# Three half-partition state copies moved from GpSimd to ScalarE in a recurrent-attention kernel

## The chip, the cores and the metric

The kernel runs on one core of a Trainium2 chip. Its time is the device time of one execution in microseconds (us). A core has five engines that run side by side and wait for each other through semaphores: TensorE (PE in the profile, with its weight loads as PEld), VectorE (DVE), ScalarE (ACT), GpSimd (POOL) and SyncE (SP), which here only issues DMAs. Each engine executes its own instructions in program order.

## The reference

A recurrence with a decaying state per batch and head runs over 768 tokens; its output, laid out as a 3072 x 384 matrix, goes through a maxout layer. Sizes: 4 batches, 8 heads, 48 numbers per head.

```python
for t in range(S):                       # _attn_ref, state is B x H x 48 x 48
    cur = np.einsum('bhd,bhe->bhde', u[None] * kt, vt)
    y[:, :, t] = np.einsum('bhd,bhde->bhe', rt, state + cur)
    state = wt[:, :, :, None] * state + np.einsum('bhd,bhe->bhde', kt, vt)

x = attn_out.transpose(0, 2, 1, 3).reshape(B * S, H * D)
out = np.maximum(x @ w1, x @ w2) @ w_out    # w1, w2: 384 x 1024, w_out: 1024 x 384
```

## The kernel before

The tokens are cut into three segments of 256. A **unit** is one or two batches at one segment: units 0 to 3 are the four batches at segment 0, one each; unit 4 is batches 0 and 1 at segment 1, unit 5 batches 2 and 3 at segment 1, units 6 and 7 the same at segment 2. A partition holds two neighbouring tokens.

For each unit `n` the steps, named as in the program, are these. `load` brings in r, k, v and the decays w by SP's queue. `wp` and `ln` form the logarithm of each pair's decay, `hi` and `lo` split it into two 16-bit parts (units 3 to 7), `ex` sums the logarithms over tokens by matmuls with a triangular matrix (the lines L380 and L381 are the two parts), `mz` adds a row's own, `e0` and `ie` are exponentials. `scale` multiplies r and k by them into `rp` and `kp`; `rw` and `kw` do the pairs' second factor. `tr` transposes these on TensorE and `te` copies the result out of PSUM into `RK` (units 5 to 7 use transposing DMAs, `dt`). `rk`, `ru`, `dg`, `dd` and `di` make the diagonal term: `rk` is the product of r and k (tile `rku`, L174 on VectorE, L178 on GpSimd, for unit 5 batch 0 on VectorE and batch 1 on GpSimd). `sc` makes scores in PSUM (L626), `mk` copies them under a mask into `M` (L635, VectorE), `ya` (L673) and `yi` (L660) make the output from the scores and from the state, `xe` copies it to `xT`.

The state: `kv` (L581) makes the segment's new key-value products in PSUM. `st.n.0` (L595 on ScalarE for segment 0, else L597 on VectorE) forms the state in the middle of the segment's pairs of halves, `st.n.1` (L600) a second sum `T`, and `sm` (GpSimd or VectorE) multiplies `T` by the decay `W` into the state for the next segment. `sb.n.e` (L606 to L610) converts the float32 state `S_f` to the bfloat16 `S_b` that `yi` uses as weights. It works on the partitions of one head of each pair: `e` = 0 is partitions 0 to 63, `e` = 1 partitions 64 to 127. So each of these copies has 64 partitions; from unit 4 on it is 768 numbers long, before that 192.

The maxout layer uses max(a, b) = b + relu(a - b): `gt` multiplies `xT` by w1 - w2 (L691), `rl` takes the relu out of PSUM into `gT` (L701 on ScalarE, L703 on VectorE), `op` adds the product with w2 w_out (L709) and that of `gT` with w_out (L713), `oe` copies the result to SBUF and `os` stores it. Units 0 to 3 have four `gt` blocks, units 4 to 7 eight.

PSUM has four banks under the tag G (`ex`, `tr`, `gt`, `op` take them in turn; a unit's `ex` keeps its bank until `scale` has read it) and two double banks under Y (`kv`, `sc`, the outputs `y`). A step that needs a bank waits for the release by the step that reads the bank's former contents.

What sets the order: the long string ORDER. Each word in it is one step, and each engine's instructions stand in the order of the words. `@a`, `@d` and `@p` name the engine of a step that can run on several: ScalarE, VectorE, GpSimd. Nothing is reordered by a scheduler; semaphore waits follow from the data.

Of the kernel before, what the change touches and what calls it, by code (L numbers as in the profile page):

```python
# [53 lines left out]
mz.0.1 e0.0.1 load.0.r rw.0.0@d ex.0.0 zero.M.1@p mz.0.0 ie.0.0 ie.0.1 kw.0.0@p identb@p wt.0.0  # L54
rw.0.1@p wt.0.1 load.1.w.0 u we.0.0 identq@a uspread hot.8.3 e0.0.0 wp.1.0@p ln.1.0 ex.1.0
zero.k.1@p rk.0.0@d utake@a ru.0.0@p load.1.r rw.1.0@p load.1.v vb.1.0@a zero.M.2@p load.0.v
scale.0.1.0.0@d scale.0.1.0.1@d scale.0.0.0.0@d tr.0.0.0 vb.0.0@a vb.0.1@a kv.0 st.0.0@a sb.0.0@p
scale.0.0.0.1@d tr.0.0.1 mz.1.0 ie.1.0 dg.0 dd.0@p we.0.1 load.1.k rk.1.0@d st.0.1 kw.1.0@d ru.1.0@d
wt.1.0 di.0.0@d te.0.0.0@a hot.8.5 sc.0.0.0.0 sc.0.0.1.0 we.1.0 vb.1.1@a te.0.0.1@a hot.8.4
sc.0.0.0.1 wload.1.2 w2turn.2.0 wload.0.1 e0.1.0 zero.M.0@p sm.0@p scale.1.0.0.0@d dg.1 load.2.w.0  # L60
# [17 lines left out]
ru.4.0@d scale.4.1.0.0@d tr.4.0.1 dg.4 sc.3.0.1.0 mk.3.0.1.0 sc.3.0.0.0 mk.3.0.0.0 oe.1.0@a  # L78
load.5.w.0 gt.2.0 rl.2.0@a load.3.v vb.3.1@a gt.2.3 rl.2.3@a gt.2.1 rl.2.1@a te.4.0.1@a vb.3.0@p
kv.3 st.3.0@a gt.2.2 scale.4.1.1.0@p kv.4 rl.2.2@a row.4 wp.5.0@p ln.5.0 hi.5@p dd.4@d di.4.0@d  # L80
di.4.1@d wl.3 load.5.r sb.3.0@a we.3 st.3.1 os.1.1 load.5.k sm.3@p os.0.1 load.5.v st.4.0 sb.4.0@p
rk.5.1@p ru.5.1@p tr.4.1.0 te.4.1.0@a tr.4.0.0 te.4.0.0@a op.0.0 tr.4.1.1 load.6.w.0 wp.6.0@p lo.5@d
st.4.1 rk.5.0@d ya.3.0.1.0 ex.5.1 ya.3.0.0.0 te.4.1.1@a sc.4.1.0.0 mk.4.1.0.0 sb.3.1@a yi.3.0
xe.3.0@a oe.0.0@a mz.5.1 ex.5.0 mz.5.0 op.2.1 oe.2.1@a sc.4.1.1.0 mk.4.1.1.0 sc.4.0.1.0 mk.4.0.1.0
# [18 lines left out]
xe.6.1@a ya.6.0.0.0 ya.6.0.1.0 op.5.0 scale.7.0.1.0@d dg.7 dt.7.0.1 xe.6.0@a gt.6.0 rl.6.0@d gt.6.1  # L103
rl.6.1@d gt.6.4 rl.6.4@a sm.5@p scale.7.1.1.0@p dt.7.1.1 scale.7.1.0.0@p gt.6.2 rl.6.2@d dd.7@d
vb.7.1@a gt.6.3 oe.5.0@a rl.6.3@a gt.6.6 gt.6.7 di.7.1@d rl.6.6@d gt.6.5 rl.6.5@d vb.7.0@a kv.7
st.7.0 sb.7.0@p sc.7.1.0.0 mk.7.1.0.0 rl.6.7@a op.6.0 sc.7.1.1.0 mk.7.1.1.0 dt.7.0.0 os.4.0 dt.7.1.0
op.6.2 sc.7.0.1.0 di.7.0@d mk.7.0.1.0 os.5.2 sc.7.0.0.0 mk.7.0.0.0 op.6.1 oe.6.1@d os.6.1 ya.7.1.0.0
ya.7.1.1.0 ya.7.0.0.0 ya.7.0.1.0 sb.7.1@a oe.6.0@d os.6.0 yi.7.0 yi.7.1 xe.7.0@a op.6.3 oe.6.3@a
os.6.3 os.5.3 os.5.0 oe.6.2@a xe.7.1@d gt.7.0 gt.7.7 rl.7.7@d rl.7.0@a gt.7.2 gt.7.1 rl.7.2@d gt.7.4
# [669 lines left out]
```

## Time and profile before

| | |
|---|---|
| three runs | 156.62, 158.8, 159.0 us; median 158.8 us |
| profiled execution, first to last instruction (span) | 156.0 us |
| its own time | not listed apart; the lowest of the runs lies 0.6 us above the span, the median 2.8 us |
| busy share of the span | PE 90%, DVE 80%, ACT 58%, POOL 58% |
| copies `S_b<-S_f` on ScalarE | 13: median 363 ns, longest 830 ns |
| copies `S_b<-S_f` on GpSimd | 3: 343, 817 and 1543 ns |

A row of the timeline gives start and length in us, engine, line, operation, output and inputs, their shapes, how many instructions are merged in the row, and in brackets how long the engine had been idle and what released it. A row of the chain gives start, length, engine, output and line. The shape `64x768` is partitions by elements. L166 is a helper that makes every plain copy and conversion, so its tile names tell which step it is. PEclk is the granted clock of TensorE as a share of full speed.

### The profile page before, as it was taken

Reading aid. Unit: us, or ns where it says so; the run is one execution under the profiler, and the core shown is the slowest. Engines: PE = TensorE matmul, PEld = TensorE weight load, DVE = VectorE, ACT = ScalarE, POOL = GpSimd, SP = SyncE. Lnnn points to the kernel's source line nnn. Section 1 sums busy time; section 2 is a strip of 40 time slices with the busy share of each in tenths; the row PEclk is TensorE's granted clock in tenths of the full one; section 3 lists DMA queues with packets and bytes.
Section 4 is the critical chain, followed back from the end, with each engine's and each line's share of the span. In section 5 each row is a group of like instructions: output and inputs, shape, how many; then the busy total and the mean of one; then the engine's idle time right before and its main releaser. Section 6 shows DMA issues by size and latency. Waiting matters only on the chain.

```text
span 156.0 us, 5548 instructions
## 1 busy us (share of the span) xinstructions
PE 140.7 (90%) x2401; PEld 85.9 (55%) x2404; DVE 124.1 (80%) x161; ACT 90.0 (58%) x165; POOL 90.4 (58%) x105
## 2 busy tenths in 40 slices
PE   4899987998899989793499999999999999999991
PEld 1364645666667758561365645665556646574560
DVE  4690997999979999499989995997889987854610
ACT  3253735779979896964069689544763673023111
POOL 7949389891734975599529579486099932000000
PEclk9999999999999999999779999999999999999998
DMA  4999997999999679996098399869989298024033
GB/s 107 305 299 365 312 327 234 326 284 344 266 244 280 169 175 334 220 254 190 1 218 238 66 194 237 228 182 152 264 195 252 52 135 200 4 103 153 0 128 131
DMA packets 71187, 31.85 MB, mean 204 GB/s; under 512 B 66293, under 2 KB 70390, under 8 KB 71162
## 3 DMA queue, kind: packets, MB, share of 16 engines
q1 hardware_dynamic: 71162, 31.49, 77.3%
q8 instruction: 19, 0.31, 0.9%
q14 instruction: 6, 0.05, 0.1%
HBM read 23.61 MB, written 4.73 MB: 182 GB/s over the span
## 4 chain that ended last, share of the span: by engine, by line
PE 63%; DVE 16%; ACT 6%; issue 5%; POOL 5%; DMA 3%; SPq 1%; DVEq 0%; POOLq 0%; ACTq 0%
PE G L691 19%; PE G L713 16%; PE G L709 7%; DVE rku L174 6%; PE Y L626 4%; PE G L232 3%; PE Y L673 3%; DMA lr<-in_r_dram 3%; DVE M L635 2%; PE Y L660 2%; ACT RK L166 2%; PE Y L581 2%; POOL wst L200 1%; PE G L305 1%; POOL kp L174 1%
## 5 line engine op out<-in xcount | busy, mean ns | idle before, releaser
L691 PE MATMUL G<-xT,wd_sb 128*128 128x256 bf16 (+1 forms) x192 | 35.3, 335 | 0.7 <-ACT xT L166 0.7
L713 PE MATMUL G<-wo_sb,gT 128*128 128x384 bf16 x192 | 35.1, 326 | 0.0
L635 DVE CAST_PREDICATED M<-mask,Y 128x1024 bf16<-128x1024 int32 (+1 forms) x26 | 28.9, 1135 | 3.7 <-PE Y L626 3.6
L701 ACT ACTIVATE gT<-G 128x512 bf16<-128x512 f32 x37 | 21.0, 603 | 18.4 <-PE G L691 18.4
L691 PEld LDWEIGHTS <-wd_sb 128*128 128x128 bf16 x192 | 18.8, 101 | 13.6 <-DVE M L501 0.7
L713 PEld LDWEIGHTS <-gT 128*128 128x128 bf16 x192 | 18.7, 98 | 12.5 <-ACT gT L701 0.2
L178 POOL TENSOR_TENSOR kp<-lk,iE 128x384 bf16<-128x384 f32 x16 | 18.2, 1161 | 8.3 <-issue 4.0
L232 PE MATMUL G<-S_b 128*128 128x512 bf16 x45 | 14.6, 469 | 2.2 <-DVE S_b L261 2.1
L178 POOL TENSOR_TENSOR rku<-rku,u_b 128x384 f32<-128x384 f32 x14 | 14.0, 1025 | 4.0 <-DVE rku L174 2.2
L166 ACT COPY osb<-G 128x384 f32<-128x384 f32 x17 | 8.1, 481 | 13.7 <-PE G L713 13.4
L709 PE MATMUL G<-wc_sb,xT 128*128 128x384 bf16 x72 | 15.7, 328 | 0.0
L166 ACT CAST xT<-Y 128x768 bf16<-128x768 f32 x10 | 10.1, 1020 | 9.8 <-PE Y L660 8.2
L174 DVE TENSOR_TENSOR rku<-lr,lk 128x768 f32<-128x768 f32 x9 | 15.3, 1712 | 0.0
L626 PE MATMUL Y<-RK 48*64 48x128 bf16 x384 | 9.8, 226 | 5.1 <-DVE M L635 4.5
L166 ACT COPY RK<-G 128x1024 bf16<-128x1024 bf16 x12 | 12.0, 1026 | 1.7 <-PE G L550 1.6
L626 PEld LDWEIGHTS <-RK 48*64 48x64 bf16 x384 | 6.3, 108 | 10.5 <-issue 9.9
L425 DVE TENSOR_TENSOR MZ<-G,lg 128x384 f32<-128x384 f32 (+1 forms) x13 | 6.7, 521 | 6.0 <-PE G L383 5.1
L174 DVE TENSOR_TENSOR rp<-lr,G 128x768 bf16<-128x768 f32 (+2 forms) x13 | 10.5, 824 | 0.9 <-ACT G L421 0.6
L487 DVE TENSOR_REDUCE dg<-rku 128x16 f32<-128x768 f32 x12 | 11.0, 946 | 0.0
L178 POOL TENSOR_TENSOR lk<-lk,lw 128x384 f32<-128x384 f32 x6 | 7.3, 1226 | 5.5 <-DVE rku L174 5.5
L703 DVE TENSOR_SCALAR gT<-G 128x512 bf16<-128x512 f32 x11 | 7.4, 690 | 3.8 <-PE G L691 3.8
L232 PEld LDWEIGHTS <-S_b 128*128 128x128 bf16 x48 | 5.0, 114 | 9.6 <-issue 4.4
(102 smaller groups left out, 241.1 us busy)
## 6 DMA issues: line engine op xcount, KB each, us to landing
lk<-in_k_dram SPq DMA_DIRECT2D x12, 384.0 KB, 5.8
lr<-in_r_dram SPq DMA_DIRECT2D x12, 384.0 KB, 6.4
lv<-in_v_dram SPq DMA_DIRECT2D x12, 384.0 KB, 6.4
out_dram<-osb SPq DMA_DIRECT2D x24, 192.0 KB, 2.1
lw<-in_w_dram SPq DMA_DIRECT2D x11, 384.0 KB, 5.1
gT<-in_moe_w_dram SPq DMA_DIRECT2D x4, 512.0 KB, 6.0
wso<-in_moe_w_out_dram SPq DMA_DIRECT2D x4, 384.0 KB, 6.0
wst<-in_moe_w_dram SPq DMA_DIRECT2D x2, 512.0 KB, 5.6
```

Of the source, the lines that this page charges most:

```text
L166: (nc.scalar.copy if e == "a" else nc.vector.tensor_copy if e == "d" else nc.gpsimd.tensor_copy)(o, i)
L174: op(o, a, b)
L178: op(o[:, g], a[:, g], b[:, g])
L232: nc.tensor.matmul(t, zz[:, 0:P], zz[:, 0:512], start=True, stop=True)
L487: nc.vector.reduce_sum(s.dg[:, b].rearrange("p i h -> p h i"), s.rku[:, b], axis=AX.X)
L626: nc.tensor.matmul(t[q * Q:(q + 1) * Q, e, p * P:(p + 1) * P].rearrange("s (i g) -> s i g", i=2), s.kT[d, b, j, y * n + p, q, :], s.rT[d, ...
L635: nc.vector.copy_predicated(t[:, :, 2 * n * y:2 * n * (y + 1)].rearrange("s i (p e) g -> s p e i g", e=2), mask[:, j].bitcast(I32).unsquee ...
L691: nc.tensor.matmul(t[:, m * n * P:(m + 1) * n * P].rearrange("c (b t) -> c b t", t=P), wd_sb[:, ko, fo * P:(fo + 1) * P], s.xT[:, 0:n, ko, :],
L701: nc.scalar.activation(o, i, AF.Relu)
L703: nc.vector.tensor_scalar_max(o, i, 0.0)
L709: nc.tensor.matmul(t[:, 0:HD], s.xT[:, a, ko, :], wc_sb[:, ko, :], start=(ko == 0), stop=False)
L713: nc.tensor.matmul(t[:, 0:HD], s.gT[:, c:c + P], wo_sb[:, f, :], start=False, stop=(f == FO - 1))
```

## The change

In ORDER the engine of `sb.0.0`, `sb.4.0` and `sb.7.0` is `@a` instead of `@p`. All other words, and their places, stay. `sb.0.1`, `sb.4.1` and `sb.7.1`, the same copies of the other 64 partitions, were on ScalarE already.

```diff
-scale.0.1.0.0@d scale.0.1.0.1@d scale.0.0.0.0@d tr.0.0.0 vb.0.0@a vb.0.1@a kv.0 st.0.0@a sb.0.0@p
+scale.0.1.0.0@d scale.0.1.0.1@d scale.0.0.0.0@d tr.0.0.0 vb.0.0@a vb.0.1@a kv.0 st.0.0@a sb.0.0@a
...
-di.4.1@d wl.3 load.5.r sb.3.0@a we.3 st.3.1 os.1.1 load.5.k sm.3@p os.0.1 load.5.v st.4.0 sb.4.0@p
+di.4.1@d wl.3 load.5.r sb.3.0@a we.3 st.3.1 os.1.1 load.5.k sm.3@p os.0.1 load.5.v st.4.0 sb.4.0@a
...
-st.7.0 sb.7.0@p sc.7.1.0.0 mk.7.1.0.0 rl.6.7@a op.6.0 sc.7.1.1.0 mk.7.1.1.0 dt.7.0.0 os.4.0 dt.7.1.0
+st.7.0 sb.7.0@a sc.7.1.0.0 mk.7.1.0.0 rl.6.7@a op.6.0 sc.7.1.1.0 mk.7.1.1.0 dt.7.0.0 os.4.0 dt.7.1.0
```

GpSimd's queue around `sb.4.0`, at the start of unit 5. The rows are, in turn, `hi.5` (output in the tile `wst`), `sm.3`, `sb.4.0`, and the GpSimd half of `rk.5` and `ru.5`; "x2" is one step in two instructions:

```order
 L200 TENSOR_SCALAR wst<-lg 128x768 [waits PE_49,Activation_49]
 L174 TENSOR_TENSOR S_f<-T,W 128x192 [waits DVE_49,Activation_49]
-L166 CAST S_b<-S_f 64x2x8x48 [waits DVE_49]
 L178 TENSOR_TENSOR rku<-lr,lk 128x384 [waits DMAHW7_49,DMAHW4_49]
 L178 TENSOR_TENSOR rku<-lr,lk 128x384
```

The copy of 64 partitions between `sm.3` and `rk.5.1` is gone; `rk.5.1` now stands right behind `sm.3`.

ScalarE's queue at the same place of the program. The rows are `sb.3.0`, `we.3` (the exponential that gives the decay `W`), the copy, the three `te.4` evictions into `RK`, and `sb.3.1`:

```order
 L166 CAST S_b<-S_f 64x4x48 [waits Activation_49]
 L473 ACTIVATE W<-WL 128x4 [waits DMAHW2_49]
+L166 CAST S_b<-S_f 64x2x8x48 [waits DVE_49]
 L166 COPY RK<-G 128x4x256 [waits PE_49] x3
 L166 CAST S_b<-S_f 64x4x48
```

`sb.4.0` now stands ahead of the three evictions and waits for VectorE's `st.4.0`.

ScalarE's queue around `sb.7.0`, where unit 6 ends its maxout and unit 7 has its new state. The rows are an `rl.6`, `vb.7.0` (the conversion of v), the copy `sb.7.0`, `rl.6.7`, `sb.7.1`, `xe.7.0` and an `oe`:

```order
 L701 ACTIVATE gT<-G 128x512 [waits PE_49]
 L166 CAST vp_77<-lv 128x8x2x48
+L166 CAST S_b<-S_f 64x2x8x48 [waits DVE_49]
 L701 ACTIVATE gT<-G 128x512 [waits PE_49]
-L166 CAST S_b<-S_f 64x2x8x48 [waits DVE_49]
+L166 CAST S_b<-S_f 64x2x8x48
 L166 CAST xT<-Y 128x6x2x64 [waits PE_49]
 L166 COPY osb<-G 128x384 [waits DMAHW3_49,DMAHW6_49,DVE_49,PE_49]
```

`rl.6.7` now stands behind a copy that waits for VectorE's `st.7.0`; before, it stood ahead of that wait.

## Prediction

> **What bounds the kernel now.** I read the chain that ended last first, for the engine that carries it; then the windows over the places where it leaves TensorE; then the timelines of the engines there.
>
> ```profile
> span 156.0 us, 5548 instructions
> ```
>
> The chain of waits in order of time (start, length, step). The pieces from 79.83 on are also my durations for TensorE at full clock:
>
> ```profile
> 68.13 6.77 DVE rku L174
> 74.90 1.14 DVE M L635
> 76.08 0.52 PE Y L626 x16
> 76.60 2.67 PE G L691 x12
> ...
> 79.83 1.42 PE G L691 x12
> 81.24 0.35 PE Y L673 x32
> 81.60 0.79 PE Y L660 x48
> 82.39 0.59 PE G L709 x3
> ...
> 90.25 0.63 PE Y L581 x64
> ...
> 151.44 1.31 PE G L713 x8
> ```
>
> From 76.08 to 152.75 the chain is TensorE's own work without a break: what delays or advances it there moves the end one for one. Before 76.08 stands one odd piece, a product on VectorE that took 6.77 us. The windows (length, busy time of each engine, granted clock) show what it does to TensorE:
>
> ```profile
> core 0: us, PE busy (x) PEld busy (x) DVE busy (x) ACT busy (x) POOL busy (x), PEclk, DMA share, GB/s
> 71.60:76.08 4.48, 0.01 (x3) 0.00 (x0) 4.48 (x3) 1.01 (x2) 3.58 (x5) 1.00 0.25 71
> 76.27:79.68 3.41, 3.41 (x44) 2.13 (x35) 2.95 (x4) 0.97 (x2) 0.67 (x1) 0.50 0.26 67
> ```
>
> TensorE stands for 4.48 us, and then works for 3.41 us at half clock. [...]
>
> Why the product is so long is read from the two queues, GpSimd's first, then VectorE's:
>
> ```profile
> 66.34 0.50 POOL L174 TENSOR_TENSOR S_f<-T,W 128x192 f32<-128x192 f32 x1
> 66.80 1.54 POOL L166 CAST S_b<-S_f 64x768 bf16<-64x768 f32 x1
> 68.31 1.96 POOL L178 TENSOR_TENSOR rku<-lr,lk 128x384 f32<-128x384 f32 x2
> ...
> 72.13 1.95 POOL L178 TENSOR_TENSOR lg<-lw 128x384 f32<-128x384 f32 x2
> 74.98 1.96 POOL L178 TENSOR_TENSOR lk<-lk,lw 128x384 f32<-128x384 f32 x2 [0.90 <-DVE rku L174]
> ```
>
> ```profile
> 66.40 1.26 DVE L398 SCALAR_TENSOR_TENSOR wst<-lg,wst 128x768 f16<-128x768 f32 x1 [2.27 <-POOL wst L200]
> 67.58 0.55 DVE L600 TENSOR_TENSOR T<-Y,S_f 128x384 f32<-128x384 f32 x1
> 68.05 6.85 DVE L174 TENSOR_TENSOR rku<-lr,lk 128x768 f32<-128x768 f32 x1
> ```
>
> ```profile
> L174 DVE TENSOR_TENSOR rku<-lr,lk x9: 947/955/6848, 7.7 to 113.2; 128x768 f32<-128x768 f32 x9
> L178 POOL TENSOR_TENSOR kp<-lk,iE x16: 987/999/1722, 28.8 to 125.3; 128x384 bf16<-128x384 f32 x16
> ```
>
> The product takes 0.955 us as a rule. Here it starts at 68.05, inside `sb.4.0`; GpSimd then runs six products without a gap until 72.13 + 1.95 = 74.08, and VectorE ends 0.82 us later, at 74.90. So it was shut out until GpSimd fell idle, which it did only because `kw.5` waits for this very product. [...]
>
> Elsewhere VectorE is not shut out so. Two pairs of products on GpSimd, each with the VectorE product that arrived during the pair's first:
>
> ```profile
> 56.07 2.78 POOL L178 TENSOR_TENSOR kp<-lk,iE 128x384 bf16<-128x384 f32 x2 [0.99 <-ACT iE L445]
> 56.23 1.76 DVE L174 TENSOR_TENSOR kp<-lk,iE 128x768 bf16<-128x768 f32 x1
> 80.91 2.68 POOL L178 TENSOR_TENSOR kp<-lk,iE 128x384 bf16<-128x384 f32 x2 [3.97 <-issue]
> 81.02 1.70 DVE L174 TENSOR_TENSOR rku<-rku,u_b 128x768 f32<-128x768 f32 x1
> ```
>
> Undisturbed, a pair takes 1.96 us. Here it takes 0.7 to 0.8 more, and VectorE about 0.75 to 0.8 more than its 0.955: it waits for the first product to end and goes next, and the second product waits for it. At 66.40 it also got in (between `sm.3`, which ends at 66.84, and `sb.4.0`, which took 1.54 instead of the 0.83 of a copy of that size). The one arrival that failed came during `sb.4.0`, the only GpSimd instruction in these rows that works on 64 partitions.
>
> [...]
>
> [...]
>
> **The change, part by part.** Three copies leave GpSimd and enter ScalarE, where the same copy of 768 numbers takes 0.83 us (a row below) and delays the next start by about 0.72.
>
> *At `sb.4.0`, GpSimd and VectorE.* `rk.5.1` follows `sm.3` directly. `lo.5` (66.40) still meets `sm.3`, gets in at 66.84 as before and ends at 67.66; `rk.5.1`'s first product is held until then and ends near 68.5. VectorE's `rk.5.0` arrives at 68.05 during this product, like the two arrivals above, gets in at 68.5 and ends near 69.3, **5.6 us earlier**. GpSimd saves the copy and pays one more hold of 0.8, so it is free at 74.0, as before.
>
> *TensorE behind it.* TensorE's last row ahead of its stand, which ends at 71.61:
>
> ```profile
> 71.19 0.42 PE L626 MATMUL Y<-RK 48*64 48x128 bf16 x16
> ```
>
> It then waits for `mk.4.1.0.0` (L635 at 74.90), which frees a double bank. That mask copy would now run from 69.3 to 70.4, before TensorE gets there, and the two `mz` after it end at 71.3. So TensorE goes on at 71.61 at full clock: scores 0.35, `gt` 1.33 to 1.42, scores 0.35, `gt` 1.42, `ya` 0.35, `yi` 0.79, in all 4.7. It would begin `op.3.0` at 76.3 instead of 82.39: **6.1 us**, of which 4.5 are the stand and 1.6 the half clock. What could be late next: the next `mk` needs scores that end at 71.6, and the four mask copies follow at 1.14 each: 72.8, 74.0, 75.1, each just ahead of the step that needs its bank (73.3, 75.1, 75.4). I take off 0.1 for these near meetings: 6.0.
>
> *What must move along.* VectorE, ScalarE and SP's queue (whose next row store waits for `mz.5`) follow these steps. GpSimd moves less: `kw.5` from 74.0 to 75.9, then four `kp` of 1.0, one conversion of v of 0.8 and two holds of 0.8: 82.3. `kv.5` needs them; TensorE comes to it at 90.25 - 6.0 = 84.2. So 1.9 us stay spare.
>
> *At `sb.4.0`, ScalarE*, with VectorE's `st.4.0` ahead:
>
> ```profile
> 63.59 0.55 DVE L597 TENSOR_TENSOR S_f<-Y,S_f 128x384 f32<-128x384 f32 x1
> ```
>
> ```profile
> 64.24 0.22 ACT L473 ACTIVATE W<-WL 128x4 f32<-128x4 f32 x1
> 64.58 1.93 ACT L166 COPY RK<-G 128x1024 bf16<-128x1024 bf16 x2
> 67.26 1.01 ACT L166 COPY RK<-G 128x1024 bf16<-128x1024 bf16 x1 [0.75 <-PE G L550]
> ```
>
> `st.4.0` is done at 64.14, so the new copy starts at 64.46 and the two evictions move by about 0.7. The third had waited 0.75 for TensorE: the delay ends there. Cost nothing; without that idle time it would be 0.7 for the evictions alone.
>
> *At `sb.0.0`.* ScalarE is without a gap here:
>
> ```profile
> 16.66 0.53 ACT L445 ACTIVATE iE<-MZ 128x384 f32<-128x384 f32 x1
> 19.39 0.52 ACT L421 ACTIVATE G<-G 128x384 f32<-128x384 f32 x1
> ```
>
> ```profile
> 20.13 0.55 DVE L174 TENSOR_TENSOR rp<-lr,G 128x384 bf16<-128x384 f32 x1
> 24.22 0.56 DVE L425 TENSOR_TENSOR MZ<-G,lg 128x384 f32<-128x384 f32 x1 [1.02 <-PE G L383]
> ```
>
> All of it moves by some 0.4. `e0.1.0` then ends at 20.3 instead of 19.9, and VectorE's `rp` starts 0.2 later; its idle 1.02 ahead of 24.22, which waits for another cause, takes that up. Cost nothing; at most the 0.4 if that idle time were not there.
>
> *At `sb.7.0`.*
>
> ```profile
> 128.61 0.62 ACT L701 ACTIVATE gT<-G 128x512 bf16<-128x512 f32 x1
> 130.33 0.83 ACT L166 CAST S_b<-S_f 64x768 bf16<-64x768 f32 x1 [1.10 <-DVE S_f L597]
> ```
>
> ```profile
> 130.29 1.46 PE L713 MATMUL G<-wo_sb,gT 128*128 128x384 bf16 x8
> ```
>
> `rl.6.7`, at 128.61 before, now waits for `sb.7.0`: start 130.33 + 0.72 = 131.05, end 131.67. It feeds the last of `op.6.0`'s eight matmuls, which started at 130.29 + 7 x 0.16 = 131.4 with its weights a little earlier. TensorE stands for **0.4 us**, and nothing behind gives it back. `sb.7.1` ends at 132.5, long before `yi.7`.
>
> **Sum**: 156.0 - 6.0 + 0.4 = 150.4 us of span. The runs lie 0.6 to 3.0 above the profiled span; the median 158.8 becomes 158.8 - 5.6 = **153.2**, the lowest 156.62 becomes 151.0.
>
> **Rivals.**
>
> *Shut out all the same.* If the cause lies in the two `rku` products or in a full GpSimd queue, and not in the copy, `rk.5.0` waits until GpSimd ends its six products. These end near 73.3 (one copy less, `lo.5`'s hold kept), so it ends 0.8 earlier. TensorE gains 0.8 and pays 0.4: 158.4. For it: six boundaries passed without letting VectorE in. Against it: both pairs above.
>
> *Something late takes part of the gain.* The mask copies or GpSimd's `kp` come late by 2 to 4 us in all: 155.2 to 157.2. Against it: the spare times above.
>
> *Slower: `lo.5` is shut out.* Without the copy, `sm.3` is followed by products. If VectorE does not get in at 66.84, it waits until GpSimd is idle at 66.8 + 6 x 0.96 = 72.6. Then `lo.5` ends at 73.4, and `ex.5.1` on TensorE, which needs it, stands from 67.7 (where `lo.5` ended before). The 3.9 us of work up to 71.6 would start at 73.4, 3.4 us of it at half clock: end 79.0, then 4.6 to `op.3.0` at 83.6 instead of 82.39. With 0.4 for `rl.6.7`: +1.6, 160.4; with a second such wait beyond 162. It decides at the end of `sm.3`. Against it: the same arrival got in before.
>
> **Chances.** Full gain 0.68 (own range 150.4 to 154.6); part of the gain 0.10; shut out all the same 0.12; `lo.5` shut out or other losses 0.10. A range from 150.4 to 158.5 takes in the first three cases and leaves about 0.15 out. About 2% is what a measurement of this kernel can tell from no change: faster takes the first case and a little of the second, 0.70; slower takes half of the last and a reserve for waits that I don't see, 0.09; the rest, 0.21, is the same.
>
> **What the profile after would show.** Right: `rk.5.0` about 1.7 us long, the first two GpSimd products of unit 5 about 0.7 longer each, no stand of TensorE near 72, no window at half clock there, and ScalarE's `rl.6.7` behind a copy near 125 with TensorE's short stand after it. Wrong: a VectorE product of several us at this place, or a new stand of TensorE in the stretch I moved as a whole.

## The result, and the profile after

| | before | changed |
|---|---|---|
| runs, us | 156.62, 157.66, 158.8, 159.0 | 152.03, 152.13, 152.38, 152.89 |
| median, us | 158.23 | 152.25 |
| profiled span, us | 156.0 | 150.3 |

The ratio of the times is 0.966, with a 95% interval from 0.959 to 0.973. A second series of the changed kernel gave a median of 151.73 and a ratio of 0.961 (0.954 to 0.969). Here and below, medians are of all runs, and ratios of the fast runs alone, those at most 1.5% above the fastest of their kernel in that series.

The page's first line of the changed kernel, and the window (length, busy time of each engine, granted clock) in which TensorE stood before:

```profile
span 150.3 us, 5551 instructions
```

```profile
core 0: us, PE busy (x) PEld busy (x) DVE busy (x) ACT busy (x) POOL busy (x), PEclk, DMA share, GB/s
71.60:76.40 4.80, 4.80 (x153) 3.76 (x146) 4.57 (x5) 4.40 (x7) 4.80 (x6) 1.00 1.00 249
```

TensorE now works through it at full clock. Its timeline there (start, length), up to the first matmuls of `op.3.0`:

```profile
71.41 0.64 PE L626 MATMUL Y<-RK 48*64 48x128 bf16 x32
71.99 1.48 PE L691 MATMUL G<-xT,wd_sb 128*128 128x256 bf16 x12
...
76.31 0.66 PE L709 MATMUL G<-wc_sb,xT 128*128 128x384 bf16 x3
```

In the profile before, the first twelve `gt` matmuls took 2.74 us instead of 1.48, and `op.3.0` started at 82.32 instead of 76.31:

```profile
76.53 2.74 PE L691 MATMUL G<-xT,wd_sb 128*128 128x256 bf16 x12
82.32 0.66 PE L709 MATMUL G<-wc_sb,xT 128*128 128x384 bf16 x3
```

The queues of VectorE and GpSimd at the same place:

```profile
66.65 1.26 DVE L398 SCALAR_TENSOR_TENSOR wst<-lg,wst 128x768 f16<-128x768 f32 x1 [2.26 <-POOL wst L200]
...
68.30 1.29 DVE L174 TENSOR_TENSOR rku<-lr,lk 128x768 f32<-128x768 f32 x1
```

```profile
66.59 0.50 POOL L174 TENSOR_TENSOR S_f<-T,W 128x192 f32<-128x192 f32 x1
67.05 3.39 POOL L178 TENSOR_TENSOR rku<-lr,lk 128x384 f32<-128x384 f32 x2
70.41 1.96 POOL L178 TENSOR_TENSOR rku<-rku,u_b 128x384 f32<-128x384 f32 x2
```

VectorE's product takes 1.29 us instead of 6.85. It got in between GpSimd's first and second product, and this pair on GpSimd took 3.39 instead of 1.96 because it was held twice, once by `lo.5` and once by `rk.5.0`.

The other end of the account is `sb.7.0`. ScalarE's and TensorE's timelines around `op.6.0`:

```profile
124.34 0.83 ACT L166 CAST S_b<-S_f 64x768 bf16<-64x768 f32 x1 [1.60 <-DVE S_f L597]
125.08 0.59 ACT L701 ACTIVATE gT<-G 128x512 bf16<-128x512 f32 x1
```

```profile
124.30 1.75 PE L713 MATMUL G<-wo_sb,gT 128*128 128x384 bf16 x8
```

The eight matmuls take 1.75 us instead of 1.46: the last waits for `rl.6.7`, which stands behind the copy.

The last eight matmuls, before and then after, end TensorE's work:

```profile
151.28 1.46 PE L713 MATMUL G<-wo_sb,gT 128*128 128x384 bf16 x8
```

```profile
145.63 1.46 PE L713 MATMUL G<-wo_sb,gT 128*128 128x384 bf16 x8
```

The account by the profiles: from the start of `rk.5.0` (68.05 before, 68.30 after) to `op.3.0` TensorE needs 8.0 us instead of 14.3, 6.3 less. The way up to there is 0.25 longer, and the way from `op.3.0` to the last matmul 0.36 longer (147.09 - 76.31 = 70.78 against 152.74 - 82.32 = 70.42), of which 0.3 lie in `op.6.0`. In all 5.7 us.

### The profile page after: what moved, and what is told of

Its sections match the earlier page's. It is cut to its first block, busy times and chain, and to the rows that moved or that the text cites. A ratio compares the mean times of both kernels' runs of the same rounds, so it can differ in the third digit from the quotient of the medians.

```text
span 150.3 us, 5551 instructions
## 1 busy us (share of the span) xinstructions
PE 138.8 (92%) x2404; PEld 84.3 (56%) x2404; DVE 118.5 (79%) x161; ACT 91.6 (61%) x168; POOL 89.8 (60%) x102
## 4 chain that ended last, share of the span: by engine, by line
PE 56%; DVE 18%; DMA 7%; POOL 6%; issue 5%; ACT 3%; SPq 3%; DVEq 0%; POOLq 0%; ACTq 0%
PE G L713 17%; PE G L691 16%; PE G L709 7%; DMA lr<-in_r_dram 7%; PE Y L673 4%; DVE M L635 3%; PE Y L626 3%; PE Y L660 2%; DVE dg L487 2%; PE G L232 2%; DVE rku L174 2%; SPq L357 2%; DVE kp L174 2%; DVE wst L398 2%; DVE rp L174 2%
## 5 line engine op out<-in xcount | busy, mean ns | idle before, releaser
L691 PE MATMUL G<-xT,wd_sb 128*128 128x256 bf16 (+1 forms) x192 | 34.1, 326 | 0.7 <-ACT xT L166 0.7
L691 PEld LDWEIGHTS <-wd_sb 128*128 128x128 bf16 x192 | 18.2, 98 | 13.0 <-DVE M L501 0.7
L709 PE MATMUL G<-wc_sb,xT 128*128 128x384 bf16 x72 | 15.7, 328 | 0.0
L166 ACT CAST S_b<-S_f 64x192 bf16<-64x192 f32 (+1 forms) x16 | 9.4, 589 | 1.8 <-DVE S_f L597 1.6
L174 DVE TENSOR_TENSOR rku<-lr,lk 128x768 f32<-128x768 f32 x9 | 9.7, 1092 | 0.0
L673 PE MATMUL Y<-M,vp 64*32 64x128 bf16 x768 | 9.1, 219 | 0.4 <-DVE M L635 0.4
```

What stands on the lines that cost most here:

```text
L166: (nc.scalar.copy if e == "a" else nc.vector.tensor_copy if e == "d" else nc.gpsimd.tensor_copy)(o, i)
L174: op(o, a, b)
L673: nc.tensor.matmul(lhsT=s.vp[g, b, 2 * p + e, j, m * 32:(m + 1) * 32], rhs=s.M[b, j][g, :, 2 * p + e, :], **into(s, b, q, p * 96 + (e + m) ...
L691: nc.tensor.matmul(t[:, m * n * P:(m + 1) * n * P].rearrange("c (b t) -> c b t", t=P), wd_sb[:, ko, fo * P:(fo + 1) * P], s.xT[:, 0:n, ko, :],
L709: nc.tensor.matmul(t[:, 0:HD], s.xT[:, a, ko, :], wc_sb[:, ko, :], start=(ko == 0), stop=False)
```

## Experiments

**Which of the three copies.** In the first kernel `sb.4.0` alone goes to ScalarE, in the second the other two.

```diff
 first:   st.4.0 sb.4.0@p  ->  st.4.0 sb.4.0@a
 second:  sb.0.0@p  ->  sb.0.0@a ,  sb.7.0@p  ->  sb.7.0@a
```

> Of the three copies only `sb.4.0` goes to ScalarE. My theory (the whole gain is VectorE's product `rk.5.0`, which no longer waits for GpSimd to fall idle; `sb.7.0` costs 0.4): span 149.9, 0.4 below the changed kernel's 150.3, and `op.6.0` on TensorE without a stand; median near 151.9. Rival (each copy that leaves GpSimd brings a part): 153 to 155.

> The other two copies, `sb.0.0` and `sb.7.0`, go to ScalarE; `sb.4.0` stays on GpSimd. My theory: the long wait of `rk.5.0` stays (6.8 us), TensorE stands for 4.5 us before 76 and works at half clock after it, and `sb.7.0` adds 0.4: median 158.6 beside 158.2 of the kernel before. Rival (each copy brings a part): 155 to 157.

The first had a median of 150.53 us, and 151.72 when it ran again beside the changed kernel's 151.73; its profiled spans are 148.3 and 150.1. The 148.3 comes from ahead of the change: `rk.5.0` began at 66.45 there, 1.8 earlier than in its second profile, and from it to the end it is 81.8 us in both profiles, against 82.0 in the changed kernel and 88.0 in the kernel before. All of the gain is `sb.4.0`'s. The second had a median of 158.68 beside 158.63 of the kernel before. Its ratio, 1.007 to 1.022, would be a loss of 1.1 to 3.4 us, more than the 0.4 expected; its profiled span, 156.5, is only 0.5 above that of before, half of it ahead of `rk.5.0`, and the size of the loss stays open. Its rows (VectorE's product; the two windows of stand and half clock; `op.6.0`):

```profile
68.29 6.84 DVE L174 TENSOR_TENSOR rku<-lr,lk 128x768 f32<-128x768 f32 x1
```

```profile
71.80:76.30 4.50, 0.02 (x4) 0.00 (x0) 4.50 (x3) 1.01 (x2) 3.60 (x5) 1.00 0.14 39
76.50:79.90 3.40, 3.40 (x44) 2.12 (x35) 2.95 (x4) 1.06 (x2) 0.65 (x1) 0.52 0.30 76
```

```profile
130.52 1.76 PE L713 MATMUL G<-wo_sb,gT 128*128 128x384 bf16 x8
```

Long product, stand and half clock are all there, and the stretched `op.6.0` as well. The other two copies bring nothing, and the rows show the cost that was named for `op.6.0`. In the kernel before, GpSimd had no queue behind them: after `sb.0.0` (16.82) came one conversion and then 2.19 us of idle time, after `sb.7.0` (130.36) nothing. VectorE's product that arrived at 17.05, during `sb.0.0`, took 0.96 us.

**The stand in `op.6.0`.** The changed kernel with two words exchanged:

```diff
-st.7.0 sb.7.0@a sc.7.1.0.0 mk.7.1.0.0 rl.6.7@a op.6.0
+st.7.0 sc.7.1.0.0 mk.7.1.0.0 rl.6.7@a sb.7.0@a op.6.0
```

> The changed kernel, with `sb.7.0` behind `rl.6.7` in ScalarE's queue instead of ahead of it. My theory (TensorE's stand of 0.3 to 0.4 in `op.6.0` comes from `rl.6.7` waiting behind the copy): the stand goes, median 0.3 to 0.4 below the changed kernel's 152.25, so 151.9. Rival (the stand has another cause or is made up for later): 152.25 as it was.

Median 151.76 us. ScalarE's and TensorE's rows of this kernel:

```profile
122.25 0.62 ACT L701 ACTIVATE gT<-G 128x512 bf16<-128x512 f32 x1
123.97 1.68 ACT L166 CAST S_b<-S_f 64x768 bf16<-64x768 f32 x2 [1.11 <-DVE S_f L597]
```

```profile
123.93 1.46 PE L713 MATMUL G<-wo_sb,gT 128*128 128x384 bf16 x8
```

`rl.6.7` is out of the way before the wait, and the eight matmuls take 1.46 again. The cause of the 0.3 is shown by the rows; the times alone, which scatter by 1 us within a kernel, could not tell it. The comparison of the first kernel with the changed one in the same series was expected to show it too:

> The kernel with `sb.4.0` alone on ScalarE, beside the changed kernel on the same chip. If `sb.7.0` on ScalarE costs what TensorE's stand in the changed kernel's `op.6.0` shows (0.3), this kernel is 0.3 faster than the changed one; both near 151 to 152.

> The changed kernel beside the one with `sb.4.0` alone, on the same chip: 152.2, 0.3 slower than it.

The times did not show it: the medians, 151.72 and 151.73, are equal. In the profiles `op.6.0` takes 1.46 and 1.76.

**What it is about the copy.** Four kernels put one instruction back on GpSimd at the place of `sb.4.0`, in the changed kernel; its output goes to a tile that nobody reads.

```diff
 st.4.0 sb.4.0@a  +  copy     64 partitions x 768      (first)
                  +  copy    128 partitions x 768      (second)
                  +  copy     64 partitions x 48       (third)
                  +  product  64 partitions x 384      (fourth)
```

> The changed kernel, with a copy of 64 partitions x 768 put back on GpSimd at the place of `sb.4.0`; it goes to a tile that nobody reads. Every theory that puts the gain down to that copy: `rk.5.0` again 6.8 us long, TensorE's stand and the half clock are back, time near 158.5. If the gain came from ScalarE doing the copy: 152.

> As before this, but the copy has all 128 partitions, so the same length on GpSimd and twice the data. [...] Theory B (arrival during a copy shuts VectorE out): 6.8 us and 158.5.

> The changed kernel, with a short copy of 64 partitions x 48 on GpSimd at that place, over before `rk.5.0` arrives (it then arrives during the first product of `rk.5.1`). [...] Theory B (what counts is the instruction during which it arrives): `rk.5.0` 1.3 to 1.8 us, time near 152.4.

> The changed kernel, with a product of 64 partitions x 384 on GpSimd at the place of `sb.4.0`, into a tile that nobody reads. [...] Theory B (only copies do it): `rk.5.0` 1.3 to 1.8 us; time near 152.4.

The kernel before, in the same series, took 156.06 to 159.17 us in eight runs (median of all nine 157.96) and once 738.15. GpSimd's and VectorE's rows, one kernel after the other. The first, 64 x 768 (runs 156.95 and 159.51 us):

```profile
67.33 1.54 POOL L619 CAST wso<-S_f 64x768 bf16<-64x768 f32 x1
```

```profile
68.58 6.84 DVE L174 TENSOR_TENSOR rku<-lr,lk 128x768 f32<-128x768 f32 x1
```

The second, 128 x 768 (152.4 and 152.57 us):

```profile
66.79 1.54 POOL L619 CAST wso<-S_f 128x768 bf16<-128x768 f32 x1
68.31 2.67 POOL L178 TENSOR_TENSOR rku<-lr,lk 128x384 f32<-128x384 f32 x2
```

```profile
68.05 1.11 DVE L174 TENSOR_TENSOR rku<-lr,lk 128x768 f32<-128x768 f32 x1
```

The two copies take the same 1.54 us and are interrupted by `lo.5` in the same way, and VectorE's product arrives during both. After 64 partitions it is shut out for the whole run of products, after 128 it goes next. So neither the load on GpSimd nor the arrival during a copy is the cause; the number of partitions is.

The third, 64 x 48 (median 157.11 us of eight runs):

```profile
65.01 0.94 POOL L623 CAST wso<-S_f 64x48 bf16<-64x48 f32 x1
65.91 1.96 POOL L178 TENSOR_TENSOR rku<-lr,lk 128x384 f32<-128x384 f32 x2
```

```profile
66.26 6.25 DVE L174 TENSOR_TENSOR rku<-lr,lk 128x768 f32<-128x768 f32 x1
```

Here the copy was over at 65.95, and VectorE arrived at 66.26, during a product on all 128 partitions. It was shut out all the same, for as long as the products ran: the sixth ended at 71.69, VectorE's 0.82 later, at 72.51. What the half-partition copy does outlasts it.

The fourth, a product of 64 x 384 (156.01 and 158.92 us):

```profile
66.91 1.71 POOL L616 TENSOR_TENSOR wso<-S_f 64x384 f32<-64x384 f32 x1
68.59 2.67 POOL L178 TENSOR_TENSOR rku<-lr,lk 128x384 f32<-128x384 f32 x2
```

```profile
68.16 1.29 DVE L174 TENSOR_TENSOR rku<-lr,lk 128x768 f32<-128x768 f32 x1
75.14 7.32 DVE L174 TENSOR_TENSOR rku<-rku,u_b 128x768 f32<-128x768 f32 x1
```

The time was like that of the kernel before, so it is not only copies that cost it, but the place was another: `rk.5.0` went next, in 1.29 us, and the next product of VectorE, `ru.5.0`, was shut out for 7.32 us, in a place where the other kernels don't show it (1.09 to 1.75 us there). The half-partition product lasted 1.71 us, of which some 0.75 are `lo.5`'s hold, so about as long on 64 partitions as one of 384 numbers on 128 (0.98). Why `ru.5.0` and not `rk.5.0` was shut out behind it is not shown by these runs.

**A wait on GpSimd.** The kernel before, with one tiny copy more on GpSimd that must wait until an earlier GpSimd instruction is complete on all partitions: right behind `sb.4.0`, or four products later.

```diff
 first:   st.4.0 sb.4.0@p       + copy of S_b[:, one element], waits for sb.4.0
 second:  rk.5.1@p ru.5.1@p     + copy of rku[:, one element], waits for ru.5.1
```

> The kernel before, all three copies on GpSimd, with one more instruction right behind `sb.4.0`: a copy of one element per partition out of `S_b`, which waits until `sb.4.0` is complete on all partitions. GpSimd gets more to do, not less. [...] Theory B (VectorE is shut out because it arrives during a copy, whatever comes then): no change, 158.2. Theory C (GpSimd's load is what counts): 158.2 or more.

> The kernel before, with a copy of one element per partition on GpSimd behind `ru.5.1`, which waits until `ru.5.1` is complete on all partitions; it stands four products behind `sb.4.0`. [...]

The first had a median of 151.98 us, ratio 0.969 (0.955 to 0.984). Its rows:

```profile
67.05 1.54 POOL L166 CAST S_b<-S_f 64x768 bf16<-64x768 f32 x1
68.66 0.80 POOL L624 COPY dum<-S_b 128x1 bf16<-128x1 bf16 x1
```

```profile
68.30 1.10 DVE L174 TENSOR_TENSOR rku<-lr,lk 128x768 f32<-128x768 f32 x1
```

The copy of the state is still on GpSimd, GpSimd has more to do than before, and the whole gain is there. The second had a median of 155.92 us, ratio 0.987 (0.979 to 0.994):

```profile
69.77 1.94 POOL L178 TENSOR_TENSOR rku<-rku,u_b 128x384 f32<-128x384 f32 x2
71.77 0.80 POOL L624 CAST dum<-rku 128x1 bf16<-128x1 f32 x1
```

```profile
67.58 4.94 DVE L174 TENSOR_TENSOR rku<-lr,lk 128x768 f32<-128x768 f32 x1
```

VectorE's product is shut out until the place of the wait, 71.71, and ends 0.81 later, at 72.52. Since it began 0.47 earlier than in the kernel before, this answers to 73.0 there, 1.9 ahead of its 74.9, as long as two of the six products (1.95). The wait's place sets the length of the shut-out. A tiny copy without a wait was not run; that the wait, and not just one more instruction, lets VectorE in rests on the six products that did not.

Whether the half clock goes with the shorter wait is read from TensorE's rows; it does not (line numbers here are 18 higher from the added code, so L644 makes scores and L709 is `gt`):

```profile
73.71 0.55 PE L644 MATMUL Y<-RK 48*64 48x128 bf16 x16 [2.60 <-DVE M L653]
74.19 2.74 PE L709 MATMUL G<-xT,wd_sb 128*128 128x256 bf16 x12
```

TensorE stood for only 2.60 us, and the twelve matmuls took 2.74 all the same.

**The half clock by itself.** The kernel before, with 16 matmuls more on TensorE in the time for which it stood; nobody reads their result.

```diff
-sc.4.1.1.0 mk.4.1.1.0 sc.4.0.1.0
+sc.4.1.1.0 hot.16.9 mk.4.1.1.0 sc.4.0.1.0
```

> The kernel before (all three copies on GpSimd, `rk.5.0` shut out as before), with 16 matmuls more on TensorE behind `sc.4.1.1.0`; their result is read by nobody, and they fill some 3.5 us of the 4.5 us for which TensorE stands. My theory of the sum (of the 6.1 us at `op.3.0`, 4.5 are the stand and 1.6 the half clock behind it): the product still ends near 74.9 and TensorE still goes on at 76.1, but at full clock, so `op.3.0` begins 1.6 earlier, near 80.7; time about 1.6 below the kernel before. Rival (half clock there has another cause or hides behind VectorE): `op.3.0` at 82.4 and no change.

The median of ten runs was 156.34 us, 0.8 below the 157.11 of the kernel before; the ratio was 0.983 (0.976 to 0.990), a gain of 1.5 to 3.8 us. TensorE's rows (15 of the 16 matmuls are in the profile):

```profile
70.94 3.63 PE L232 MATMUL G<-S_b 128*128 128x512 bf16 x15
75.51 0.42 PE L626 MATMUL Y<-RK 48*64 48x128 bf16 x16 [0.95 <-DVE M L635]
75.86 1.48 PE L691 MATMUL G<-xT,wd_sb 128*128 128x256 bf16 x12
77.58 0.42 PE L626 MATMUL Y<-RK 48*64 48x128 bf16 x16 [0.23 <-DVE M L635]
...
80.63 0.66 PE L709 MATMUL G<-wc_sb,xT 128*128 128x384 bf16 x3
```

With TensorE busy, the twelve `gt` matmuls behind the wait take 1.48 us instead of 2.74: the half clock is gone. From the start of `rk.5.0` (67.47) to `op.3.0` it is 13.16 us instead of 14.27, so 1.1 earlier, not 1.6. At full clock TensorE runs up to VectorE's mask copies, as the wait of 0.23 at 77.58 shows. In the changed kernel, where these come early, this loss doesn't occur.

How long the half clock lasts differs between executions with the same long wait. The kernel with the short added copy (64 x 48), from the end of TensorE's last matmul before its stand on (the granted clock is the third number from the right):

```profile
69.80:71.80 2.00, 0.00 (x0) 0.00 (x0) 2.00 (x1) 0.99 (x2) 1.89 (x2) 1.00 0.40 115
71.80:73.70 1.90, 0.00 (x2) 0.00 (x1) 1.90 (x3) 0.00 (x0) 1.11 (x2) 0.50 0.04 10
73.70:78.60 4.90, 4.90 (x50) 3.23 (x50) 4.10 (x5) 2.04 (x3) 0.85 (x1) 0.50 0.54 141
```

Here the clock fell 2.0 us after the last matmul, inside the stand, and 4.9 us of work ran at half clock, as in the kernel with the 64 x 768 copy. In the kernel before it fell only when TensorE had begun again, and 3.4 us of work were slow. What sets the moment isn't shown by these runs.

## Why the prediction was right, by its steps

**The long wait of `rk.5.0`.** It was forecast to end near 69.3, and ended at 69.59 after a start 0.25 later; its length and the 3.39 us of GpSimd's pair are those of an arrival that goes next, 1.3 and two holds. (The prediction's list of signs said about 1.7 us, which does not follow from its own 68.05 to 69.3.) That the copy's 64 partitions were the cause was an inference from a single case. The half and full copies show that it is the number of partitions, the short copy that the effect outlasts the instruction, and the two added waits that it ends where GpSimd waits for its own earlier instruction. `rk.5.0` took 1.1 to 1.3 us when it went next, and 4.9 to 6.9 us when it was shut out behind a half-partition instruction with further products queued. What keeps it out for so long, no run shows.

**TensorE behind it.** Forecast: 6.1, less 0.1; measured from profile to profile at `op.3.0`: 82.32 - 76.31 = 6.0. Counted from the start of the product it is 6.3, since the changed kernel came there 0.25 later. The stand was 4.5 of it, and the rest, 1.8, is near the 1.6 set down for the half clock; taken alone, the half clock was worth 1.1. The size of this term was in part luck: in the two profiles where the half clock covers 4.9 us of work it would be larger (from `rk.5.0` to `op.3.0` it is 14.9 us with the 64 x 768 copy, against 14.3 in the kernel before, after stands of 4.43 and 4.47). How long a stand must be for the clock to fall is not shown; half clock stood behind stands of 4.47 us in the kernel before and 2.60 in the one with the later wait, and full clock behind 0.95 with TensorE kept busy. The steps that were to follow did: the three masks behind the scores run at 71.88 in one row, and nothing on TensorE waits for GpSimd later.

**ScalarE at `sb.4.0`** and **at `sb.0.0`.** At `sb.4.0` the copy ran at 64.60 and the delay of the evictions ended before TensorE's work. At `sb.0.0` VectorE's idle time ahead of the `MZ` row was 1.02 before and is 0.80 now, as if the 0.2 foreseen had been taken up:

```profile
24.87 0.56 DVE L425 TENSOR_TENSOR MZ<-G,lg 128x384 f32<-128x384 f32 x1 [0.80 <-PE G L383]
```

But it was 0.69 in the second profile of the kernel with `sb.4.0` alone, where `sb.0.0` is on GpSimd, so the row does not show it. The start of the program scatters more than that: `rk.5.0` began between 66.3 and 68.6 in these profiles, with and without the copy on ScalarE, so a cost of some tenths there stays open.

**`sb.7.0`.** Forecast 0.4, measured 0.3 in `op.6.0`; with `rl.6.7` ahead it is gone.

**Sum and rivals.** The span came out at 150.3 where 150.4 was forecast. The median, 152.25, lies 0.95 below the forecast 153.2. The term that was off is the median to start from: 158.8 came from three runs, and a fourth made it 158.23, which is 0.57 of the 0.95. The rest is that the medians moved by 5.98 and not 5.6, more than the 5.7 of the profiles. The prediction had set the profiled execution of before 2.8 below the median; in the later runs of both kernels, whose spans are listed, time less span is about 1.8, so that execution stands for about 157.8.

The rival in which VectorE is shut out all the same, by the products or by GpSimd's full queue, is refuted: both are in the changed kernel, and `rk.5.0` took 1.29 us. It was shut out again only when a copy of 64 partitions was put back. The slower rival, `lo.5` shut out, did not come: `lo.5` took 1.26 us as before, behind `sm.3`, which has all partitions.

## What to carry to other kernels

When an instruction of VectorE is several times as long as its like, look at GpSimd's queue beside it: here the cost of one 0.8 us copy was 6 us, because it had half the partitions and a queue without waits stood behind it. Such a copy can go to another engine (152.25 us here) or be followed by something that waits for it (151.98). A copy on all partitions did no harm either (152.49 as an added instruction); `sb.4.0` itself was not run that way. And on an engine that works in order, put a step that waits for news behind the step that others already wait for: that is the 0.3 us of `sb.7.0`.

## What the runs showed that I had not expected

The fourth extra instruction, a product on 64 partitions, let the first VectorE product through and shut out a later one for 7.32 us. So the damage can appear 8 us behind the instruction that was added, at one that has nothing to do with it; why it came there is not shown. And a short copy of 48 numbers, 0.94 us with its wait for `lo.5`, was nearly as harmful as one of 768 (6.25 us against 6.84).

The fastest of these kernels by their rows are the one with `sb.4.0` alone on ScalarE (medians 150.53 and 151.72 us) and the one with `sb.7.0` behind `rl.6.7` (151.76): 81.8 us from `rk.5.0` to the end, against 82.0 in the changed kernel. They have neither the long wait nor the stand in `op.6.0`, but their times don't separate from those of the changed kernel.

The half clock is not a fixed price of the long wait: in the kernel before the clock fell some 4.7 us after TensorE's last matmul, and 3.4 us of work were slow; in the one with the 64 x 48 copy it fell after 2.0 us, and 4.9 were slow.
